# Seven-product blocks in chains of one PSUM bank, and tile 7's second layer in seven products

## Chip, cores and metric

The kernel runs on one core of a Trainium2 chip. The metric is device time in microseconds (us). Of before there are three runs: 278.85, 278.99 and 279.15, median 278.99. A separate profiled execution of it took 279.09 us; its trace spans 277.3 us, counted from the span's start.

## What is computed

Inputs are q, k, v of shape (8, 8, 576, 64) (batch, head, row, depth) and two weight matrices of 512x2048 and 2048x512, all float32.

```python
q_s = softmax(q, axis=-1); k_s = softmax(k, axis=2)
kv  = einsum('bhsd,bhse->bhde', k_s, v)
x   = einsum('bhsd,bhde->bhse', q_s, kv) -> (4608 tokens, 512)
h   = x @ w_in
out = maximum(0.01 * h, h) @ w_out          # (4608, 512)
```

## The kernel before

The 4608 tokens are nine tiles of 512 (TT). xT holds x transposed in bf16, tokens along the free axis. For a tile, layer 1 makes 16 blocks of 128 hidden features: four matmuls (line 562) into a PSUM bank, then `leaky` on ACT (line 571), which writes g in bf16. Layer 2 takes, for each of the tile's four groups of 128 tokens (tsub), 16 matmuls of 512 columns (line 583); ACT copies the bank out and SP issues two stores (`store`, line 575). The attention of the next batches is threaded into tiles 0 to 6 by hooks: `at(t, u, ...)` registers work at step u of tile t, `run(t, u)` emits it. The order on each engine is the order in which the program emits its instructions; engines meet by semaphores alone, and each engine works its queue in order.

The last two tiles, TA = 7 and TB = 8 (counted from 0), are done together after tile 6's layer 1. Seen as two token halves (tile 7, tile 8), two halves of the 512 inputs (CL, CR) and two halves of the 2048 features, layer 1 is a 2x2 by 2x2 block product, and is made with seven products of sums in place of eight (Winograd's form). `token_sums` (line 831) makes s1 to s4 on DVE and a22 on ACT; `in_weight_sums` (line 809) makes t1 to t4 and b22 for each of eight blocks on POOL. All sums and their products are float32r (fp32r in the profile), the plain blocks bf16.

`pair_layer1(i)` (line 978) does block i of eight (NH), features i and 8 + i of both tiles. A product (`product`, line 964) is two matmuls of 512 columns into a PSUM bank of its own. `pair_first` (line 973) makes the first, and ACT copies it out as e1 (line 976). Seven additions on DVE (`add`, line 988) join banks and SBUF partial sums: u2 = p6 + e1, u3 = p7 + u2, e1 + p2, u4 = p5 + u2, c22 = p5 + u3, u3 + p4, u4 + p3. Each of the four results goes through `leaky`. g of tile 7 goes to `g7` (two gj tiles and, from i = 2, places in xT that are no longer needed, `spent`), g of tile 8 to `g8`, also in xT.

Between the products stand `fill` matmuls (`between(n)`, line 1048): 48 matmuls of tile 6's layer 2 and then 16 `pair_step` (line 1023), matmuls of tile 7's layer 2. A block has 14 matmuls of products and 8 fills. After block 7 the other 48 pair steps run (line 1076), while DVE makes the sums r1 to r4 of tile 8's g (lines 1070 to 1074) and ACT copies c22 (line 1069). ACT then copies out and SP stores tile 7. Tile 8's layer 2 is again made in seven products (`product2`, line 1082): 16 matmuls of 256 columns each, the first two bf16, five fp32r with v1 to v4 and o22, sums of w_out made earlier. Its seven additions are at line 1100. Stores (`put`, line 1108) are issued by SP and ACT.

PSUM has eight banks: psB_pool six (tag bank2k), psO_pool two (tag pout).

Of the kernel before, what the change touches and what calls it, by code (L numbers as in the profile page):

```python
# [26 lines left out]
def kernel(  # L27
# [39 lines left out]
    qT_pool = front.enter_context(tc.tile_pool(name="qT", bufs=2))  # L67

# [48 lines left out]
    qe1 = const_pool.tile([P, XE.stop, P], BF16, name="qe1")  # L117
    vb2 = [const_pool.tile([P, R, 2, 2, D + 2], BF16, name=f"vb{i}") for i in range(2)]
# [678 lines left out]
    def out_weight_tiles():  # L797
        for n in ("v1", "v3", "v2", "v4", "o22"):
            late[n] = strip(n).rearrange("p a b -> p (a b)")[:, 0 : NH * H2].rearrange("p (m o) -> p m o", o=H2)
# [9 lines left out]
    def in_weight_sums(i):  # L809
        w = lambda cs, fh: w_in_sb[:, cs, (fh * NH + i) * P : (fh * NH + i + 1) * P]  # L810
        if i == 0:
            late["t"] = strip("t")
# [18 lines left out]
    def token_sums():  # L831
        front.close()
        late["one"] = pool = pairs.enter_context(tc.tile_pool(name="late", bufs=1, reuse_waits="tile"))
# [128 lines left out]
    g8 = spent  # L962

    def product(w, a):
        ps = psB_pool.tile([P, TT], FP32, name="pp", tag=BANK_TAG)
        for c in range(2):
            nc.tensor.matmul(ps, lhsT=w(c), rhs=a(c), start=(c == 0), stop=(c == 1))  # L967
        return ps

    of = lambda n: (lambda c: late[n][:, c])  # L970
    firsts, held_leaky = {}, []

    def pair_first(i):
        firsts[i] = e1 = late["pool"].tile([P, TT], FP32, name="e1")
        ps = product(lambda c: w_in_sb[:, c, i * P : (i + 1) * P], lambda c: xT[:, c, XA])
        nc.scalar.copy(out=e1, in_=ps)

    def pair_layer1(i):
        e1 = firsts[i]
        u2, c22 = (late["one"].tile([P, TT], FP32, name=n) for n in ("u2", "c22"))  # L980
        u3, u4 = (late["pool"].tile([P, TT], FP32, name=n) for n in ("u3", "u4"))
        if i < 2:
            pair = g_pool.tile([P, 2, TT], BF16, name="gj")
            g7[i], g7[NH + i] = pair[:, 0], pair[:, 1]
        else:
            g7[i], g7[NH + i] = (spent(NF + 2 * (i - 2) + n) for n in range(2))

        def add(o, ps, e):
            nc.vector.tensor_tensor(out=o, in0=ps, in1=e, op=ALU.add)  # L989

        p6 = product(of(("t2", i)), of("s2"))
        p7 = product(of(("t3", i)), of("s3"))
        between(2 if i == 0 else 3)
        add(u2, p6, e1)
        for fn in held_leaky:
            fn()
        add(u3, p7, u2)
        p2 = product(lambda c: w_in_sb[:, 2 + c, i * P : (i + 1) * P], lambda c: xT[:, 2 + c, XA])
        add(e1, p2, e1)
        leaky(g7[i], e1)  # L1000
        if i + 1 < NH:
            pair_first(i + 1)
        between(1 if i == 0 else 2)
        p5 = product(of(("t1", i)), of("s1"))
        p4 = product(of(("t4", i)), of("a22"))
        p3 = product(of(("b22", i)), of("s4"))
        between(2 if i == 0 else 3)
        add(u4, p5, u2)
        add(c22, p5, u3)
        if i == 0:  # L1010
            nc.gpsimd.tensor_copy(out=gate, in_=c22[:, 0:1])
        leaky(g8(NH + i), c22)
        add(u3, p4, u3)
        leaky(g8(i), u3)
        add(u4, p3, u4)
        held_leaky[:] = [lambda: leaky(g7[NH + i], u4)]
        if i + 2 < NH:
            in_weight_sums(i + 2)

    pouts, started = {}, [0] * NTS  # L1020
    turn = [j for i in range(NH) for j in (i, NH + i)]

    def pair_step(tsub):
        j = turn[started[tsub]]
        started[tsub] += 1
        if tsub not in pouts:
            pool, tag = (psO_pool, "pout") if tsub < 2 else (psB_pool, BANK_TAG)
            pouts[tsub] = pool.tile([P, O], FP32, name="pout", tag=tag)
        nc.tensor.matmul(  # L1029
            pouts[tsub],  # L1030
            lhsT=g7[j][:, tsub * P : (tsub + 1) * P],
            rhs=w_out_sb[:, j],
            start=(started[tsub] == 1),
            stop=(started[tsub] == NF),
        )
# [17 lines left out]
    between(3)  # L1053
    for i in range(NH):
        pair_layer1(i)
    held_leaky[0]()
    next(fill, None)
    pairs.close()
    pool = ctx.enter_context(tc.tile_pool(name="late3", bufs=1, reuse_waits="tile"))
    quarter = lambda h, b, fh: xT[:, :, (2 * fh + b) * TT + h * M2 : (2 * fh + b) * TT + (h + 1) * M2]  # L1060
    for n in ("r1", "r2", "r3", "r4", "c22"):
        late[n] = pool.tile([P, NH, M2], F32R, name=n)
    for first in (True, False):
        for b in range(2):
            o = lambda n: late[n][:, 4 * b : 4 * b + 4]
            part = lambda n: o(n).bitcast(FP32)
            a11, a12, a21, a22 = (quarter(h, b, fh) for h in range(2) for fh in range(2))
            if first:
                nc.scalar.copy(out=o("c22"), in_=a22)
                nc.vector.tensor_tensor(out=o("r1"), in0=a21, in1=a22, op=ALU.add)  # L1070
                nc.vector.tensor_tensor(out=o("r2"), in0=part("r1"), in1=a11, op=ALU.subtract)
            else:
                nc.vector.tensor_tensor(out=o("r3"), in0=a11, in1=a21, op=ALU.subtract)
                nc.vector.tensor_tensor(out=o("r4"), in0=a12, in1=part("r2"), op=ALU.subtract)

    while started[0] < NF:
        for tsub in range(NTS):
            pair_step(tsub)
    for tsub in range(NTS):
        store(TA * TT + tsub * P, pouts[tsub], nc.scalar.copy)  # L1080

    def product2(a, w, each=False):
        if each:
            ps = [psB_pool.tile([P, H2], FP32, name="pq", tag=BANK_TAG) for _ in range(2)]
        else:
            both = psB_pool.tile([P, 2, H2], FP32, name="pq", tag=BANK_TAG)
            ps = [both[:, 0], both[:, 1]]
        for i in range(2):
            for m in range(NH):
                nc.tensor.matmul(  # L1090
                    ps[i],
                    lhsT=a(m)[:, i * P : (i + 1) * P],
                    rhs=w(m),
                    start=(m == 0 and (each or i == 0)),
                    stop=(m == NH - 1 and (each or i == 1)),
                )
        return ps if each else both

    def add(o, ps, e):
        nc.vector.tensor_tensor(out=o, in0=ps, in1=e, op=ALU.add)  # L1100

    rows = lambda n: (lambda m: late[n][:, m])
    plain_g = lambda fh: (lambda m: g8(fh * NH + m)[:, 0:M2])
    plain_w = lambda fh: (lambda m: w_out_sb[:, fh * NH + m, E1])
    out1, out2 = ([osb_pool.tile([P, O], FP32, name="out_sb") for _ in range(2)] for _ in range(2))
    e1, u2, u3, u4 = (g_pool.tile([P, 2, H2], FP32, name="gu", tag="gj") for _ in range(4))

    def put(o, half, i, cols):
        for n, issue in enumerate((nc.sync, nc.scalar)):
            b, c = divmod(TB * TT + half * M2 + i * P + n * L, S)  # L1110
            issue.dma_start(out=out_r[b, c // L, :, cols], in_=o[n * L : (n + 1) * L, cols])

    nc.scalar.copy(out=e1, in_=product2(plain_g(0), plain_w(0)))
    ps = product2(plain_g(1), plain_w(1))
    for i in range(2):
        add(out1[i][:, E1], ps[:, i], e1[:, i])
        put(out1[i], 0, i, E1)
    add(u2, product2(rows("r2"), rows("v2")), e1)
    add(u3, product2(rows("r3"), rows("v3")), u2)
    ps = product2(rows("r1"), rows("v1"))  # L1120
    for i in range(2):
        add(out2[i][:, E2], ps[:, i], u3[:, i])
    add(u4, ps, u2)
    ps = product2(rows("c22"), rows("v4"), True)
    for i in range(2):
        add(out2[i][:, E1], ps[i], u3[:, i])
        put(out2[i], 1, i, slice(0, O))
    ps = product2(rows("r4"), rows("o22"), True)
    for i in range(2):
        add(out1[i][:, E2], ps[i], u4[:, i])  # L1130
        put(out1[i], 0, i, E2)
# [31 lines left out]
```

## Time and profile before

| what | value |
|---|---|
| median of three runs | 278.99 us |
| profiled execution | 279.09 us, span 277.3 us |
| PE busy | 270.5 us, 98% of the span |
| DVE busy | 221.7 us, 80% |
| ACT busy | 165.4 us, 60% |
| POOL busy | 75.8 us, 27% |
| granted TensorE clock | 1.0 for the whole span |

The time is that of the run; the span is what the trace shows of one execution, some 1.8 us less. PE is TensorE's matmuls, PEld its weight loads, DVE VectorE, ACT ScalarE, POOL GpSimd, SP the engine that issues most DMAs. In a row of the groups, "x32 | 21.4, 688 | 2.9" means 32 instructions, 21.4 us busy together, 688 ns each, 2.9 us idle ahead of them, and then what ended that idle time. A row of the timeline is start, length, engine, line, operation, out<-in, shape and count; "[0.26 <-PE pp L967]" is an idle time ahead of it and what ended it. The length of several pipelined instructions runs from the first's start to the last's end, and so overlaps the next row. The chain that ended last counts from one end to the next, and its pieces don't overlap.

### The profile page before, as it was taken

What the parts mean: (1) busy time and instruction counts of PE and PEld (TensorE: products, weight loads), DVE (VectorE), ACT (ScalarE), POOL (GpSimd) and SP (SyncE); (2) the same over time, 40 slices, a digit from 0 to 9 for tenths busy, and PEclk for the clock granted to TensorE, in tenths of its full rate; (3) what the DMA queues carried; (4) which work ended last, traced back from release to release, by engine and by line L of the source; (5) the groups of instructions that cost most, each with busy time, mean ns of one, the idle gap of its engine ahead of it and who ended that gap; (6) DMA issues with size and microseconds to landing.
All of it is one profiled execution on the core that took longest, in us unless ns stands there. A gap on an engine that the chain in (4) does not pass through costs nothing.

```text
span 277.3 us, 5114 instructions
## 1 busy us (share of the span) xinstructions
PE 270.5 (98%) x1970; PEld 142.6 (51%) x1970; DVE 221.7 (80%) x310; ACT 165.4 (60%) x291; POOL 75.8 (27%) x97
## 2 busy tenths in 40 slices
PE   8799999999999999999999999999999999999994
PEld 3378644444444444445444444454445556564694
DVE  2996995999999949965886498966959998999643
ACT  4976673784489366755486438665673766655300
POOL 2857460259003003100400077003000756600000
PEclk9999999999999999999999999999999999999999
DMA  7999999986995597089408940330601011010253
GB/s 242 334 206 322 244 260 290 392 309 192 272 408 184 66 401 286 2 218 398 136 0 219 406 119 8 85 73 5 162 2 38 0 38 38 9 33 0 57 135 114
DMA packets 40167, 46.46 MB, mean 168 GB/s; under 512 B 18768, under 2 KB 23632, under 8 KB 40144
## 3 DMA queue, kind: packets, MB, share of 16 engines
q1 hardware_dynamic: 36160, 41.43, 47.6%
q0 software_dynamic: 3504, 4.20, 8.8%
q10 hardware_dynamic: 480, 0.52, 0.6%
q8 instruction: 15, 0.25, 0.3%
q14 instruction: 8, 0.07, 0.1%
HBM read 36.70 MB, written 9.44 MB: 166 GB/s over the span
## 4 chain that ended last, share of the span: by engine, by line
PE 91%; DMA 5%; POOL 2%; SPq 0%; DVE 0%; issue 0%
PE pout L583 35%; PE ph L562 33%; PE pp L967 9%; PE pout L1029 5%; PE pq L1090 5%; DMA w_in_sb<-in_moe_w_in_dram 3%; DMA k_raw<-in_k_dram 2%; PE po L478 1%; PE pokv L340 1%; POOL w_in_sb L132 1%; PE pkv L340 1%; POOL vb L217 0%; POOL qe L272 0%; SPq L83 0%; PE pokv L478 0%
## 5 line engine op out<-in xcount | busy, mean ns | idle before, releaser
L583 PE MATMUL pout<-w_out_sb,gj 128*128 128x512 bf16 x448 | 102.6, 380 | 0.0
L562 PE MATMUL ph<-xT,w_in_sb 128*128 128x512 bf16 (+1 forms) x512 | 98.8, 353 | 0.1
L571 ACT ACTIVATE gj<-ph 128x512 bf16<-128x512 f32 x112 | 63.5, 602 | 19.1 <-PE ph L562 18.5
L562 PEld LDWEIGHTS <-w_in_sb 128*128 128x128 bf16 x512 | 49.6, 98 | 47.4 <-DMA w_in_sb<-in_moe_w_in_dram 0.3
L583 PEld LDWEIGHTS <-gj 128*128 128x128 bf16 x448 | 42.1, 98 | 51.5 <-issue 3.5
L217 POOL CAST vb<-v_raw 128x1152 bf16<-128x1152 f32 x13 | 21.1, 1650 | 83.0 <-DMA v_raw<-in_v_dram 83.0
L577 ACT COPY out_sb<-pout 128x512 f32<-128x512 f32 x28 | 16.1, 587 | 41.5 <-PE pout L583 19.2
L320 DVE TENSOR_REDUCE qsum<-qe 128x36 f32<-128x2304 bf16 (+5 forms) x13 | 20.1, 1542 | 6.4 <-ACT qe L311 6.2
L989 DVE TENSOR_TENSOR u<-pp,u 128x512 f32<-128x512 f32 x32 | 21.4, 688 | 2.9 <-PE pp L967 1.3
L205 ACT ACTIVATE ke<-k_raw 128x2304 bf16<-128x2304 f32 (+2 forms) x13 | 18.0, 1383 | 8.2 <-DVE k_raw L197 7.8
L327 DVE TENSOR_TENSOR qe<-qe,qrec 128x2304 bf16<-128x2304 bf16 (+5 forms) x13 | 21.6, 1660 | 0.5
L244 DVE TENSOR_REDUCE qmax<-q_raw 128x36 f32<-128x2304 f32 (+5 forms) x13 | 19.9, 1539 | 0.0
L311 ACT ACTIVATE qe<-q_raw 128x2304 bf16<-128x2304 f32 (+5 forms) x13 | 17.2, 1322 | 3.9 <-POOL q_raw L303 3.0
L197 DVE TENSOR_TENSOR k_raw<-k_raw,kall 128x1152 f32<-128x1152 f32 (+2 forms) x10 | 18.1, 1821 | 0.3
L303 POOL TENSOR_TENSOR q_raw<-q_raw,qmax 128x512 f32<-128x512 f32 (+3 forms) x7 | 11.8, 1680 | 20.5 <-DVE qmax L244 19.3
L967 PE MATMUL pp<-s,t 128*128 128x512 f32 x48 | 16.9, 458 | 0.0
L159 DVE TENSOR_TENSOR t<-t 128x256 f32<-128x256 f32 (+2 forms) x22 | 14.3, 652 | 0.7
L360 DVE RECIPROCAL krec<-pokv 128x2 f32<-128x2 f32 x8 | 1.3, 165 | 16.4 <-PE pokv L478 16.4
L499 ACT CAST xT<-po 128x448 bf16<-128x448 f32 (+3 forms) x31 | 13.3, 515 | 1.3 <-PE po L478 1.3
L789 POOL TENSOR_TENSOR t<-w_in_sb 128x256 fp32r<-128x256 bf16 x16 | 11.4, 715 | 7.6 <-PE pp L967 7.6
L303 DVE TENSOR_TENSOR q_raw<-q_raw,qmax 128x2304 f32<-128x2304 f32 (+1 forms) x6 | 13.2, 2202 | 0.2
L159 DVE TENSOR_TENSOR t<-k_raw 128x512 f32<-128x512 f32 (+1 forms) x11 | 11.2, 1017 | 0.8 <-DMA k_raw<-in_k_dram 0.6
(118 smaller groups left out, 297.4 us busy)
## 6 DMA issues: line engine op xcount, KB each, us to landing
out_dram<-out_sb SPq DMA_DIRECT2D x66, 128.0 KB, 2.8
q_raw<-in_q_dram SPq DMA_DIRECT2D x6, 1152.0 KB, 8.9
v_raw<-in_v_dram SPq DMA_DIRECT2D x6, 1152.0 KB, 11.9
k_raw<-in_k_dram SPq DMA_DIRECT2D x5, 1152.0 KB, 6.7
k_raw<-in_k_dram SPq DMA_DIRECT2D x6, 576.0 KB, 6.0
v_raw<-in_v_dram SPq DMA_DIRECT2D x4, 576.0 KB, 7.6
w_in_sb<-in_moe_w_in_dram POOLq DMA_DIRECT2D x7, 256.0 KB, 7.6
w_out_sb<-in_moe_w_out_dram POOLq DMA_DIRECT2D x6, 256.0 KB, 9.1
```

What stands on the lines that cost most here:

```text
L159: nc.vector.tensor_tensor(out=o, in0=i0, in1=i1, op=ALU.max)
L197: eng.tensor_tensor(out=ks, in0=ks, in1=st[b]["kall"][:, hs].unsqueeze(2).to_broadcast([P, n, R, D]), op=ALU.subtract,)
L217: eng.tensor_copy(out=o, in_=i)
L244: nc.vector.tensor_reduce(out=o, in_=st[b]["q"][:, hs, rs], axis=AX.X, op=ALU.max)
L303: eng.tensor_tensor(out=qs, in0=qs, in1=st[b]["qmax", rs.start, hs.start].unsqueeze(3).to_broadcast([P, m, n, D]), op=ALU.subtract,)
L320: nc.vector.reduce_sum(out=qsum, in_=q_cols(b, rs, hs), axis=AX.X)
L327: nc.vector.tensor_tensor(out=qes if out is None else out, in0=qes, in1=st[b]["qrec", rs.start, hs.start].unsqueeze(3).to_broadcast([P, n, ...
L562: nc.tensor.matmul(ph, lhsT=w_in_sb[:, cb, j * P : (j + 1) * P], rhs=xT[:, cb, c0 : c0 + n], start=(cb == 0 and first), stop=(cb == NB - 1 ...
L571: nc.scalar.activation(out=o, in_=ph, func=AF.Prelu, alpha=LEAKY_SLOPE)
L583: nc.tensor.matmul(pout, lhsT=g_sb[j // 2][:, j % 2, tsub * P : (tsub + 1) * P], rhs=w_out_sb[:, j, os], start=(j == 0), stop=(j == NF - 1),)
L967: nc.tensor.matmul(ps, lhsT=w(c), rhs=a(c), start=(c == 0), stop=(c == 1))
L989: nc.vector.tensor_tensor(out=o, in0=ps, in1=e, op=ALU.add)
```

## The change

Layer 1 of tiles 7 and 8: the products of a block accumulate in PSUM. One bank (px) takes the first, sixth, seventh and fourth product one after another; its partial sums are copied out after the first (e1, ACT), the sixth (u2, DVE) and the seventh (u3, DVE), and the last is read by `leaky` directly. A second bank (py) takes the fifth and the third product. Three additions are left: e1 + pw, u3 + py, u2 + py; the last is held over into the next block. The fills are tile 6's 48 matmuls alone: two ahead, 1 + 2 + 1 in block 0, 2 + 2 + 2 in the others.

Layer 2 of tile 7 has no pair steps any more. It is made in seven products, in turns with those of tile 8, each tile with chains of the same kind: copies by ACT (`snap`), three additions of 256-column halves by DVE. r1 and r3 of tile 7 are summed ahead by POOL (DVE for the last rows), the other row sums by DVE in the end stage, c22 by ACT. The order is written out: first of both tiles, second of both, sixth, fifth, seventh of tile 7, sixth of tile 8, fourth, third of tile 7, seventh, fifth, fourth, third of tile 8.

For room in SBUF qe1 and vb move to a pool that ends with the attention, a pool "late0" for r3 and r1 is opened ahead of the others, and t takes the first strip of the raw pool.

```diff
-    qe1 = const_pool.tile([P, XE.stop, P], BF16, name="qe1")
+    qe1 = fix_pool.tile([P, XE.stop, P], BF16, name="qe1")
...
+    def sums_ahead(n):
...
+        (ms, h0), (_, h1) = g7_blocks(0)[n], g7_blocks(1)[n]
+        for name, x, y, op in (("r1", h1(0), h1(1), ALU.add), ("r3", h0(0), h1(0), ALU.subtract)):
+            eng = nc.vector if n == 3 else nc.gpsimd
+            eng.tensor_tensor(out=late[name][:, ms], in0=x, in1=y, op=op)
...
+    def product(ps, w, a, first=True):
         for c in range(2):
-            nc.tensor.matmul(ps, lhsT=w(c), rhs=a(c), start=(c == 0), stop=(c == 1))
+            nc.tensor.matmul(ps, lhsT=w(c), rhs=a(c), start=(first and c == 0), stop=(c == 1), skip_group_check=True)
...
+    def pair_layer1(i, fills):
+        px, e1 = firsts[i]
...
+        product(px, of(("t2", i)), of("s2"), False)
+        for fn in held:
+            fn()
+        nc.vector.tensor_copy(out=u2, in_=px)
+        pw = bank()
+        product(pw, lambda c: w_in_sb[:, 2 + c, i * P : (i + 1) * P], lambda c: xT[:, 2 + c, XA])
+        if i + 1 < NH:
+            pair_first(i + 1)
+        add(e1, pw, e1)
+        leaky(g7[i], e1)
+        between(fills[0])
+        product(px, of(("t3", i)), of("s3"), False)
+        nc.vector.tensor_copy(out=u3, in_=px)
+        py = bank()
+        product(py, of(("t1", i)), of("s1"))
+        between(fills[1])
+        add(u3, py, u3)
+        leaky(g8(NH + i), u3)
...
+        product(px, of(("t4", i)), of("a22"), False)
+        leaky(g8(i), px)
+        between(fills[2])
+        product(py, of(("b22", i)), of("s4"), False)
+        held[:] = [lambda: add(u2, py, u2), lambda: leaky(g7[NH + i], u2)]
         if i + 2 < NH:
             in_weight_sums(i + 2)
+        if i in (2, 4, 6):
+            sums_ahead(i // 2 - 1)
...
-        for tsubs in ((2, 3), (0, 1)):
-            for _ in range(4):
-                for tsub in tsubs:
-                    pair_step(tsub)
-                    yield
...
+    def snap(z, n):
+        z[n] = gu()
+        if z["each"]:
+            for i in range(2):
+                nc.scalar.copy(out=z[n][:, i], in_=z["x"][i])
+        else:
+            nc.scalar.copy(out=z[n], in_=z["xx"])
...
+    def sixth(z):
+        product2(z["x"], rows("r2"), rows("v2"), z["each"], first=False)
+        snap(z, "u2")
...
+    first(A)
+    sums(A, "r2")
+    first(B8)
+    sums(A, "r4")
+    sums(A, "c22")
+    second(A)
+    c11(A)
+    second(B8)
+    sixth(A)
+    fifth(A)
+    late["r1"] = strip("r1").rearrange("p a b -> p (a b)")[:, 0 : NH * M2].rearrange("p (m t) -> p m t", t=M2)
+    for (ms, _), (_, h1) in zip(g8_wide(0), g8_wide(1)):
+        nc.vector.tensor_tensor(out=late["r1"][:, ms], in0=h1(0), in1=h1(1), op=ALU.add)
+    c11(B8)
+    sums(B8, "r2")
+    seventh(A)
+    A["o2"], B8["o2"] = out_pairs(), last_pairs("o2")
+    sixth(B8)
+    c22(A)
+    fourth(A)
+    sums(B8, "c22")
+    third(A)
+    sums(B8, "r3")
+    seventh(B8)
+    fifth(B8)
+    c12(A)
+    sums(B8, "r4")
+    c22(B8)
+    fourth(B8)
+    third(B8)
+    c12(B8)
```

In the new code A is tile 7 and B8 tile 8.

More of the change, by code (lines that the diff above doesn't have):

```diff
@@ L973, in pair_first @@
+    firsts, held = {}, []
     def pair_first(i):
-        firsts[i] = e1 = late["pool"].tile([P, TT], FP32, name="e1")
-        ps = product(lambda c: w_in_sb[:, c, i * P : (i + 1) * P], lambda c: xT[:, c, XA])
+        ps, e1 = bank(), keep("e1")
+        product(ps, lambda c: w_in_sb[:, c, i * P : (i + 1) * P], lambda c: xT[:, c, XA])
         nc.scalar.copy(out=e1, in_=ps)
[L978 to L995, printed above, removed]
-            fn()
[L997 to L1000, printed above, removed]
@@ L1052 @@
     pair_first(0)
-    between(3)
+    between(2)
     for i in range(NH):
-        pair_layer1(i)
-    held_leaky[0]()
+        pair_layer1(i, (2, 2, 2) if i else (1, 2, 1))
+    for fn in held:
+        fn()
     next(fill, None)
+    sums_ahead(3)
     pairs.close()
[L1059 to L1062, printed above, removed]
@@ L1099, in add @@
[L1099 to L1111, printed above, removed]
@@ L1113 @@
[L1113 to L1131, printed above, removed]
+    last_pool = ctx.enter_context(tc.tile_pool(name="late3", bufs=1, reuse_waits="tile"))
+    def banks2(each=False, pool=psB_pool, tag=BANK_TAG):
+        if each:
+            return [pool.tile([P, H2], FP32, name="pq", tag=tag) for _ in range(2)]
+        both = pool.tile([P, 2, H2], FP32, name="pq", tag=tag)
+        return [both[:, i] for i in range(2)]
@@ new lines, in product2 @@
+    def product2(ps, a, w, each=False, turns=False, first=True):
+        order = [(i, m) for i in range(2) for m in range(NH)]
+        if turns:
+            order = [(i, m) for m in range(NH) for i in range(2)]
+        for i, m in order:
+            nc.tensor.matmul(
+                ps[i],
+                lhsT=a(m)[:, i * P : (i + 1) * P],
+                rhs=w(m),
+                start=(first and m == 0 and (each or i == 0)),
+                stop=(m == NH - 1 and (each or i == 1)),
+                skip_group_check=True,
+            )
@@ new lines, in second, with fifth, seventh, fourth @@
+    def second(z):
+        z["w"] = banks2(False, psO_pool, "pout")
+        product2(z["w"], plain_g(z["g"], 1), plain_w(1), turns=True)
+    def sixth(z):
+        product2(z["x"], rows("r2"), rows("v2"), z["each"], first=False)
+        snap(z, "u2")
+    def fifth(z):
+        z["y"] = banks2(z["each"])
+        product2(z["y"], rows("r1"), rows("v1"), z["each"])
+    def seventh(z):
+        product2(z["x"], rows("r3"), rows("v3"), z["each"], first=False)
+        snap(z, "u3")
+    def fourth(z):
+        product2(z["x"], rows("c22"), rows("v4"), z["each"], first=False)
+        for i in range(2):
+            nc.scalar.copy(out=z["o2"][i][:, E1], in_=z["x"][i])
+            put(z, z["o2"][i], 1, i, slice(0, O))
@@ new lines, in third, with c11, c22, c12 @@
+    def third(z):
+        product2(z["y"], rows("r4"), rows("o22"), z["each"], first=False)
+    def c11(z):
+        for i in range(2):
+            add(z["o1"][i][:, E1], z["w"][i], z["e1"][:, i])
+            put(z, z["o1"][i], 0, i, E1)
+    def c22(z):
+        for i in range(2):
+            add(z["o2"][i][:, E2], z["y"][i], z["u3"][:, i])
+    def c12(z):
+        for i in range(2):
+            add(z["o1"][i][:, E2], z["y"][i], z["u2"][:, i])
+            put(z, z["o1"][i], 0, i, E2)
+    def sums(z, n):
+        pool = late["ahead"] if n == "r3" else last_pool
+        row_sums(z["wide"], n, n, pool, *dict(
+            r2=(ALU.subtract, "r1", (0, 0)),
+            r3=(ALU.subtract, (0, 0), (1, 0)),
+            r4=(ALU.subtract, (0, 1), "r2"),
+            c22=(None, (1, 1), None),
+        )[n])
```

137 lines of the change are left out of this document (72 added, 65 removed).

## The prediction

> **What bounds the kernel now.** I read the chain that ended last first, then the windows of the end, then the rows of single engines. The chain is nearly all PE:
>
> ```profile
> PE 91%; DMA 5%; POOL 2%; SPq 0%; DVE 0%; issue 0%
> ```
>
> Windows for the four stretches the change touches: block 0 of tile 8's layer 1, blocks 1 to 7, the rest of tile 7's layer 2, the seven products of tile 8's layer 2. Columns: stretch, its length, busy time and count of PE, PEld, DVE, ACT, POOL, then granted clock, DMA share, GB/s.
>
> ```profile
> 210.84:215.59 4.75, 4.72 (x22) 2.63 (x20) 4.64 (x7) 1.26 (x4) 0.00 (x0) 1.00 0.24 55
> 215.59:249.49 33.90, 33.90 (x153) 20.00 (x151) 31.17 (x50) 21.68 (x39) 17.92 (x31) 1.00 0.10 24
> 249.49:260.51 11.02, 11.02 (x53) 5.04 (x52) 10.85 (x11) 4.46 (x7) 0.00 (x0) 1.00 0.01 1
> 260.51:277.30 16.79, 13.08 (x113) 12.54 (x110) 5.38 (x12) 2.03 (x4) 0.00 (x0) 1.00 0.47 125
> ```
>
> PE is busy 33.90 of 33.90 us in blocks 1 to 7 and DVE 31.17: DVE is near full, but PE never waits for it. So DVE work that goes frees nothing by itself. What can shorten the end is less PE work; what can lengthen it is a PE instruction that has to wait. One block and the end in the chain (start, length, engine, tile, line, matmuls):
>
> ```profile
> 238.66 1.40 PE pp L967 x6
> 240.05 0.66 PE pout L583 x3
> 240.72 0.93 PE pp L967 x4
> 241.65 0.66 PE pout L1029 x3
> 242.31 0.86 PE pp L967 x4
> 243.18 0.43 PE pout L1029 x2
> 243.61 1.38 PE pp L967 x6
> 249.49 11.02 PE pout L1029 x51
> 260.51 13.10 PE pq L1090 x112
> ```
>
> A bf16 matmul of 512 columns takes 0.86/4 = 0.216 us of the stream (0.218 in the fills, 0.66/3), an fp32r one 0.93/4 = 0.2323. The 112 of 256 columns divide by their starts:
>
> ```profile
> 260.35 3.66 PE L1090 MATMUL pq<-w_out_sb,xT 128*128 128x256 bf16 x32
> 263.76 6.00 PE L1090 MATMUL pq<-v,r 128*128 128x256 f32 x48
> 269.60 2.08 PE L1090 MATMUL pq<-v,c 128*128 128x256 f32 x16
> ```
>
> (269.60 - 263.76)/48 = 0.121 each in fp32r, 0.108 in bf16. Seven products are therefore 32 x 0.108 + 80 x 0.1206 = 13.1 us, against 64 x 0.216 = 13.8 us for a plain layer 2.
>
> **Part 1: the PE work.** Out go 64 plain matmuls of tile 7's layer 2, 16 in the fills and 48 after them: 16 x 0.218 + 48 x 0.216 = 13.86 us. In come seven products: 13.10 us. Layer 1 keeps its 14 matmuls a block. Gain **0.76 us**, the largest that the change can bring. The fills fall from eight to six a block; a block without waits is 4 x 0.216 + 10 x 0.2323 + 6 x 0.218 = 4.50 us.
>
> **Part 2: what a wait of an fp32r matmul costs.** The chains in one bank bring waits that before did not have: a product may add to the bank only when the copy of what is there has been read. Before has one stop of this kind, at block 0, where the seventh product waited for s3 (DVE, line 789):
>
> ```profile
> 210.62 1.22 DVE L789 TENSOR_TENSOR s<-xT 128x1024 fp32r<-128x1024 bf16 x1
> 211.96 0.30 PEld L967 LDWEIGHTS pp<-s,t 128*128 128x128 f32 x2 [0.44 <-issue]
> 211.99 0.47 PE L967 MATMUL pp<-s,t 128*128 128x512 f32 x1
> ```
>
> s3 ends at 211.84; the weights, which had long been there, load only at 211.96; the matmul ends at 212.46. So the stop holds the weight load too: release 0.12 us, then 0.50 us to the end of the first matmul. Another release:
>
> ```profile
> 10.59 0.28 DVE L393 TENSOR_REDUCE kr<-kT 128x2 f32<-128x128 f32 x1
> 10.93 0.44 PE L398 MATMUL kallp<-identf,kr 128*64 128x128 f32 x4 [0.31 <-DVE kr L393]
> ```
>
> 10.93 - 10.87 = 0.06. I take 0.08, between 0.06 and 0.12: a matmul that waits ends 0.58 us after what it waits for. For 256 columns:
>
> ```profile
> 263.73 0.19 PEld L1090 LDWEIGHTS pq<-v,r 128*128 128x128 f32 x1
> 263.76 0.36 PE L1090 MATMUL pq<-v,r 128*128 128x256 f32 x1
> ```
>
> From the load's start to the matmul's end 0.39, so 0.08 + 0.39 = 0.47.
>
> **Part 3: the copies.** The trace has the same copy, PSUM to SBUF on DVE, at another line, and the add it replaces:
>
> ```profile
> L577 DVE COPY out_sb<-pout 128x512 f32<-128x512 f32 x4 | 2.5, 682 | 0.0
> L989 DVE TENSOR_TENSOR u<-pp,u 128x512 f32<-128x512 f32 x32 | 21.4, 688 | 2.9 <-PE pp L967 1.3
> ```
>
> A copy costs what an add does. DVE falls from seven such operations a block to five, which pays nothing, but two of the five now stand between two products. How soon DVE starts, and how close two follow each other:
>
> ```profile
> 243.16 0.68 DVE L989 TENSOR_TENSOR e<-pp,e 128x512 f32<-128x512 f32 x1
> 244.10 0.69 DVE L989 TENSOR_TENSOR u<-pp,u 128x512 f32<-128x512 f32 x1 [0.26 <-PE pp L967]
> 244.71 0.68 DVE L989 TENSOR_TENSOR c<-pp,u 128x512 f32<-128x512 f32 x1
> ```
>
> The fifth product is the first two of the six matmuls at 243.61 and ends at 244.07: DVE starts 0.03 later, and the next operation follows after 0.61.
>
> *u3, then the fourth product.* From the end of the seventh product: DVE starts at 0.04, ends at 0.73, the first matmul of the fourth ends at 0.73 + 0.58 = 1.31. PE's work between is the fifth product and two fills; unstopped, that matmul would end at 0.465 + 0.436 + 0.232 = 1.13. **Stop 0.18 us, eight times: 1.44.** Behind it stand the rest of the PE queue and all that comes later.
>
> *u2, then the seventh.* From the end of the block before: the held add starts at 0.04, the copy at 0.65, ends at 1.34, plus 0.58 = 1.92. Unstopped: sixth 0.465, second and next first 0.864, two fills 0.436, 0.232 = 2.00. No stop in blocks 1 to 6, by 0.08. In block 7 there is no next first (0.432): **0.35**.
>
> *u3's add, then the third.* The add ends 0.73 later than the copy, at 1.46, plus 0.58 = 2.04; the third's first matmul stands, after the stop, at 1.31 + 0.232 + 0.436 + 0.232 = 2.21. Nothing.
>
> **Block 0.** Three operations that were not in PE's way before now are:
>
> ```profile
> 210.41 0.43 PE pp L967 x2
> 210.93 0.59 ACT L976 COPY e<-pp 128x512 f32<-128x512 f32 x1
> 212.89 0.69 DVE L989 TENSOR_TENSOR u<-pp,e 128x512 f32<-128x512 f32 x1
> ```
>
> The sixth product now waits for ACT's copy e1 (to 211.52): first matmul at 212.10 where 210.84 + 0.436 + 0.232 = 211.51 was possible, **0.59**. The copy u2 stands on DVE behind s1 to s4, so where the add stood, 212.89 to 213.58: the seventh's first matmul at 214.16 against 212.33 + 0.864 + 0.218 + 0.232 = 213.64, **0.52**. The third's wait for u3's add costs **0.05**. The old wait for s3 goes: 212.46 against 211.96 + 0.232, **-0.27**.
>
> **Part 4: the end.** Tile 7 and 8 in turns are 64 bf16 and 160 fp32r matmuls. DVE has to make r2, r4 of tile 7 and r1, r2 of tile 8 before the sixth product of tile 8, at these prices:
>
> ```profile
> 252.53 1.23 DVE L1071 TENSOR_TENSOR r<-r,xT 128x1024 fp32r<-128x1024 f32 x1
> 253.67 1.22 DVE L1070 TENSOR_TENSOR r<-xT 128x1024 fp32r<-128x1024 bf16 x1
> 269.80 0.76 DVE L1100 TENSOR_TENSOR out_sb<-pq,gu 128x256 f32<-128x256 f32 x2 [1.23 <-PE pq L1090]
> ```
>
> ```profile
> L571 ACT ACTIVATE xT<-u 128x512 bf16<-128x512 f32 x14 | 8.4, 627 | 0.8 <-DVE u L989 0.8
> ```
>
> One after another they take 1.14 for 1024 elements (253.67 - 252.53), 0.61 for 512 as above, and 0.34 for 256 (0.76 for two against 0.42 for the single one at this line). From the end of layer 1: held add and leaky (0.63) to 1.43; the last r1, r3 1.21; r2 and r4 of tile 7 in pieces of 512, 1024, 512, 2.35 each; c11 0.68; r1 2.28; c11 0.68; r2 of tile 8 2.36: **13.34**. PE has done four bf16 products (6.91), three fp32r (5.79) and four matmuls (0.48) by 13.18, and the fifth would end at 13.30; it ends at 13.34 + 0.47 = 13.81: **0.51**. After that DVE stays ahead: tile 8's r3 follows 3.1 us later (13.34 + 0.68 + 2.36 = 16.4), and the product that reads it starts at about 19.0; r4 is done 2.7 us before the last product. ACT's snapshots (0.59, as for e1) have a whole product (1.93) to hide behind. POOL's six new sums are bounded by
>
> ```profile
> L272 POOL TENSOR_TENSOR qe<-qe,qrec 128x512 bf16<-128x512 bf16 x1 | 1.0, 1041 | 0.0
> 239.21 0.68 POOL L789 TENSOR_TENSOR t<-w_in_sb 128x256 fp32r<-128x256 bf16 x1 [1.91 <-PE pp L967]
> ```
>
> that is 2.1 us more in three blocks, against 1.9 us that POOL waits in each and a block of lead; without that cover block 5 or 7 would pay the difference, 0.2 us. The stores of tile 7 move into the products; what follows the last matmul (add of 256 columns, two stores a half) is the same as before. Moving qe1, vb2 and t changes only which finished tiles the late ones lie on; all readers of those come before s1 on their engines, so nothing is priced.
>
> **Sum.** -0.76 - 0.27 + 0.59 + 0.52 + 1.44 + 0.05 + 0.35 + 0.51 = **+2.4 us**. The profiled execution took 279.09 us with a span of 277.3; the median shown is 278.99, 0.1 below, and I put the sum on it: **281.4 us**. Every 0.01 us of release counts eleven times: releases of 0.03 and 0.12 give +1.9 and +2.9, 280.9 to 281.9.
>
> **Rivals.** *A, the weight load goes ahead of the wait.* Then a stopped matmul ends 0.40 (its own length) and not 0.50 after the release; the stops fall, in the order of the sum and with a release of 0.05, to 0.46 + 0.52 + 0.40 + 0.05 + 0.22 + 0.38, with none to 0.41 + 0.52 + 0 + 0.04 + 0.17 + 0.35. Less 1.03 that is +1.0 and +0.5: 279.5 to 280.0. For it: unstopped loads do run beside the matmul before. Against it: the load at 211.96. The Trainium skill, in TensorE: Matmul & The Clock Gate, section Step-by-step: what each phase is for, says that PE's queue pulls weight loads ahead of matmuls in flight when they go to the background buffer. By that rule it would be A; the one row here that shows a wait disagrees.
>
> *B, faster.* The change pays if no product finds its copy unfinished: the stop of 0.18 lies only that far over the edge, and one fill more between (0.218) would close it. Then the PE bill alone counts, and block 0 must lose its two stops as well: 278.99 - 0.76 = 278.2. It decides at a copy of 0.50 us; the row has 0.682. Against it also: block 0's 1.1 us hang on DVE's queue, not on this edge.
>
> *C, DVE's run at the end is longer.* From layer 1's end DVE works 11.9 us with no gap, and all that it loses there delays tile 8's sixth product one for one. The trace has SBUF operations of one shape at two prices:
>
> ```profile
> L159 DVE TENSOR_TENSOR t<-t 128x256 f32<-128x256 f32 x11 | 6.7, 606 | 0.3
> L303 DVE TENSOR_TENSOR q_raw<-q_raw,qmax 128x256 f32<-128x256 f32 x1 | 0.4, 425 | 0.0
> ```
>
> A tenth on 11.9 us is 1.2 us: 282.6. Against it: POOL has nothing to do then, and the r rows of before ran at one price.
>
> *D, the change doesn't do what it says:* excluded for the operations, since the built kernel has two copies and three adds a block on DVE; open only for time, which is B.
>
> **How the numbers follow.** Forecast 0.60, A 0.17, C 0.12, B 0.06, 0.05 for what I have not seen. The range takes in A and C and leaves out B: 279.5 to 282.8. About 0.2% (0.56 us) is what a measurement of this kernel tells from no change, so same is 278.43 to 279.55: the low end of A and a share of the unseen, 0.08; faster 0.07 (B and a little unseen); slower 0.85.
>
> **What would show it.** Right: blocks 4.65 to 4.7 us apart; PEld idle with "issue" before the weights of the fourth product in each block; block 0's last product near 216.6 and layer 1's near 249.3; sixth product of tile 8 waiting about half a us for DVE; span about 279.7. Wrong: blocks 4.5 apart with no idle before the fourth product (A or B); DVE copies clearly under 0.6; gaps on PE in the end other than that one; POOL's weight sums late before a sixth product.

## The result and the profile after

| | before | after |
|---|---|---|
| median | 279.02 us (278.85 to 279.15, 4 runs) | 282.59 us (281.84 to 282.73, 4 runs) |
| profiled execution, span | 279.09, 277.3 | 282.73, 280.9 |
| first matmul of the pair stage starts | 210.25 | 210.76 |
| last matmul ends | 273.61 | 276.90 |
| between the two | 63.36 | 66.14 |
| last matmul to the span's end | 3.69 | 4.00 |

After is slower by the ratio 1.0123, interval [1.0104, 1.0142]. The forecast was 281.4. The profiled execution is 3.6 us longer: **2.78** in the stretch that the change rewrites (forecast +2.4), 0.3 behind the last matmul, and 0.5 by a later start of that stretch. The last two were in no term of the sum. Spans are known to 0.1 us, so what is given behind the last matmul holds to 0.05.

The windows of after, cut at the ends of the first product, of block 0, of layer 1 and of the last matmul; the columns are those of the windows of before.

```profile
211.35:217.29 5.94, 5.30 (x22) 2.53 (x20) 4.70 (x6) 2.71 (x6) 0.78 (x2) 1.00 0.21 47
217.29:250.35 33.06, 32.91 (x141) 17.26 (x140) 22.91 (x35) 20.96 (x37) 23.73 (x36) 1.00 0.08 17
250.35:276.90 26.55, 26.45 (x224) 25.34 (x222) 19.78 (x28) 10.46 (x21) 0.00 (x0) 1.00 0.31 72
276.90:280.90 4.00, 0.00 (x0) 0.00 (x0) 0.42 (x1) 0.00 (x0) 0.00 (x0) 0.82 0.44 121
```

Blocks 1 to 7 have 12 matmuls fewer than before, in the count that the trace shows (141 against 153), and last 33.06 us against 33.90: 0.84 less, where 14 fills at 0.218 (two in each of seven blocks) would be 3.05 less. PE looks busy in 32.91 of the 33.06, for the record of a matmul that waits for its weights gets longer and counts as busy: those of the fourth product take up to 0.499 us in after, at most 0.398 in before. DVE fell from 31.17 to 22.91. Busy time does not show this loss; the places of the instructions do. One block of after in the chain that ended last:

```profile
226.29 1.81 PE pp L1012 x8
228.10 0.43 PE pout L584 x2
228.53 0.94 PE pp L1012 x4
229.46 0.45 PE pout L584 x2
229.91 0.66 PE pp L1012 x2
230.57 0.45 PE pout L584 x2
231.02 1.81 PE pp L1012 x8
```

From 226.29 to 231.02 it is 4.73 us. The four matmuls of the seventh and fifth product take 0.94, 0.235 each; the two of the fourth product take 0.66 where two take 0.465. That is the stop, **0.20** a block. Its cause stands in the timelines of DVE, PEld and PE, block 1 of after:

```profile
219.57 0.69 DVE L1043 COPY u<-pp 128x512 f32<-128x512 f32 x1 [0.35 <-PE pp L1012]
220.37 0.69 DVE L1015 TENSOR_TENSOR u<-pp,u 128x512 f32<-128x512 f32 x1
```

```profile
220.32 0.30 PEld L1012 LDWEIGHTS pp<-a,t 128*128 128x128 f32 x2 [0.37 <-DVE u L1043]
```

```profile
220.32 0.73 PE L1012 MATMUL pp<-a,t 128*128 128x512 f32 x2
```

The copy u3 ends at 220.26. The weights of the fourth product, on SBUF since long before, load 0.06 later. They do not load at the start of the two fills, at 219.84, though PEld has nothing to do for 0.37 us. The weight load waits with its matmul, so the stop holds both.

The late start comes in this execution from far ahead, from tile 0. Row of the costliest groups, after:

```profile
L563 PE MATMUL ph<-xT,w_in_sb 128*128 128x512 bf16 (+1 forms) x512 | 98.8, 352 | 0.3 <-DMA w_in_sb<-in_moe_w_in_dram 0.3
```

PE waited there for a piece of w_in. In the timelines about 31 us the second layer of tile 0 starts 0.53 later than in before (31.61 against 31.08), and all that follows keeps this:

```profile
31.08 2.11 PE L583 MATMUL pout<-w_out_sb,gj 128*128 128x512 bf16 x9
```

```profile
31.61 1.67 PE L584 MATMUL pout<-w_out_sb,gj 128*128 128x512 bf16 x7
```

It differs from execution to execution: ten other kernels of this study have the same code up to the pair stage, and their starts lie between 210.06 and 210.94. Where the profiled start was 210.76 to 210.94, that run was 0.7 to 0.9 us above the lowest of the same kernel (282.73 with 281.84 beside it; 282.75 with 282.09 to 282.15; 281.17 with 280.44 to 280.70). The piece of w_in is not the only source. After again (start 210.87) and three mends (210.94), both below, begin the second layer of tile 0 at 31.19 and 31.07, much as before does; from the start of tile 1's second layer to the first matmul of tile 2 they then take 15.66 and 15.99 where before takes 15.32, and in three mends PE waits 0.22 there for POOL (vb, line 218). What makes some executions late in tile 1, and whether the moved places have a part in it, no run here settles. What is compared below is therefore, beside the times, the stretch from the pair stage's first matmul to the last matmul, which does not depend on it.

### The profile page after: what moved, and what is told of

It is laid out like the page before. It is cut to its first block, busy times and chain, and to the rows that moved or that the text cites. A ratio compares the mean times of both kernels' runs of the same rounds, so it can differ in the third digit from the quotient of the medians.

```text
span 280.9 us, 5223 instructions
## 1 busy us (share of the span) xinstructions
PE 273.1 (97%) x2018; PEld 147.7 (53%) x2018; DVE 216.8 (77%) x303; ACT 170.2 (61%) x302; POOL 81.2 (29%) x103
## 5 line engine op out<-in xcount | busy, mean ns | idle before, releaser
L584 PE MATMUL pout<-w_out_sb,gj 128*128 128x512 bf16 x448 | 103.7, 380 | 0.0
L218 POOL CAST vb<-v_raw 128x1152 bf16<-128x1152 f32 x13 | 19.8, 1551 | 83.7 <-DMA v_raw<-in_v_dram 66.4
L578 ACT COPY out_sb<-pout 128x512 f32<-128x512 f32 x24 | 14.0, 584 | 34.8 <-PE pout L584 18.0
L1015 DVE TENSOR_TENSOR u<-pp,u 128x512 f32<-128x512 f32 x16 | 11.1, 692 | 8.6 <-PE pp L1012 7.8
L1012 PE MATMUL pp<-s,t 128*128 128x512 f32 x48 | 14.9, 419 | 0.8 <-issue 0.3
L572 ACT ACTIVATE xT<-u 128x512 bf16<-128x512 f32 x14 | 8.8, 630 | 10.9 <-DVE u L1015 10.8
```

What stands on the lines that cost most here:

```text
L218: eng.tensor_copy(out=o, in_=i)
L572: nc.scalar.activation(out=o, in_=ph, func=AF.Prelu, alpha=LEAKY_SLOPE)
L584: nc.tensor.matmul(pout, lhsT=g_sb[j // 2][:, j % 2, tsub * P : (tsub + 1) * P], rhs=w_out_sb[:, j, os], start=(j == 0), stop=(j == NF - 1),)
L1012: nc.tensor.matmul(ps, lhsT=w(c), rhs=a(c), start=(first and c == 0), stop=(c == 1), skip_group_check=True)
```

## The experiments

| kernel | median, us | ratio to before, interval | pair stage's first matmul to the last one | last matmul to span's end |
|---|---|---|---|---|
| before | 279.02 | 1 | 63.36 | 3.69 |
| after | 282.59 | 1.0123 [1.0104, 1.0142] | 66.14 | 4.00 |
| after again | 282.13 | 1.0121 [1.0106, 1.0136] | 66.13 | 4.00 |
| places only | 279.20 | 1.0010 [1.0001, 1.0019] | 63.38 | 3.74 |
| chains in layer 1 only | 280.91 | 1.0076 [1.0062, 1.0090] | 65.10 | 3.74 |
| seven products only | 281.85 | 1.0106 [1.0092, 1.0119] | 65.51 | 3.99 |
| fills 2, 3, 1 | 281.56 | 1.0095 [1.0082, 1.0109] | 65.33 | 3.99 |
| fills 2, 1, 3 | 283.74 | 1.0174 [1.0159, 1.0189] | 67.63 | 3.93 |
| s4 on POOL | 281.65 | 1.0101 [1.0084, 1.0117] | 65.58 | 4.02 |
| r4 late | 281.94 | 1.0112 [1.0097, 1.0127] | 65.79 | 3.98 |
| three mends | 280.52 | 1.0050 [1.0038, 1.0062] | 64.48 | 3.98 |
| one chain a block | 279.92 | 1.0038 [1.0023, 1.0052] | 63.60 | 3.99 |
| copy first | 278.91 | 0.9994 [0.9980, 1.0008] | 62.78 | 3.94 |

The before that runs beside each lay at 278.88 to 279.02. The theory: each stop of PE is paid by itself, since PE is the one chain, and the stops at copies cost more than the saved fills. Its rivals: the moved places, the end stage, or a weight load that does go ahead (A).

**Places only.** Before, with the three moved places alone (t's in out_weight_tiles).

```diff
-    qe1 = const_pool.tile(...)
-    vb2 = [const_pool.tile(...) for i in range(2)]
+    qe1 = fix_pool.tile(...)
+    vb2 = [fix_pool.tile(...) for i in range(2)]
...
+        late["t"] = strip("t")
```

> Before with the moved places alone: qe1 and vb in the pool that ends with the attention, t in the first strip; every product as before. In the profile of after, layer 1 of the last two tiles starts 0.51 us later than in before (first product ends at 211.35, not 210.84). Theory (the waits for copies are the cost, the late start is chance): no change, within 0.3 us of before, start near 210.8. Rival (the places delay the front part): +0.5 us, start near 211.35.

The stretch is 63.38 against 63.36; the time is 0.2 above, at the edge of what can be told. The places are not the cause of what the stretch loses.

**Chains in layer 1 only.** Before with the moved places and the new product chains in layer 1; the second layer of tile 7 stays plain, so there are eight fills a block.

```diff
...
-        pair_layer1(i)
+        pair_layer1(i, (2, 3, 3) if i else (1, 2, 2))
```

> Chains in one bank in layer 1 alone; tile 7's layer 2 stays plain, so each block has eight fills, 2 + 3 + 3. Theory: the third fill (0.22) covers the stop of 0.18 to 0.20 ahead of the fourth product, so blocks 1 to 6 run at 4.93 us as before; left are the stops of block 0 (0.37 + 0.52 + 0.18 + 0.05 - 0.27 = 0.85) and of block 7 (0.35): +1.2 us. Rival (chains cost by themselves, in matmuls that add to a bank or in releases that fills don't cover): 4.93 + 0.2 us a block, +2.5 us or more.

The stretch grows by 1.74, more than the 1.2 expected and less than the 2.5 of the rival. One of blocks 1 to 6, in the chain that ended last:

```profile
226.22 1.80 PE pp L981 x8
228.02 0.43 PE pout L584 x2
228.45 0.93 PE pp L981 x4
229.38 0.66 PE pout L584 x3
230.05 0.47 PE pp L981 x2
230.52 0.67 PE pout L584 x3
231.19 1.81 PE pp L981 x8
```

With three fills ahead of it the fourth product takes 0.47: no stop. The blocks are 4.97 apart, 4.95 in before (238.66 to 243.61). So a third fill covers the copy, and what is left of the cost lies in block 0 (about 1.0, expected 0.85) and in block 7, where the seventh product waits 0.6 us for the copy u2 (expected 0.35). That copy starts at 247.44, when the second product ends, and not 0.61 after the held addition (246.57), as it does in after (245.72 and 246.33); why, no run shows. The chains alone cost 1.9 us of time and bring nothing to PE.

**Seven products only.** Layer 1 as in before, seven banks and seven additions, but with six fills; the new end.

```diff
-        between(2 if i == 0 else 3)
+        between(1 if i == 0 else 2)
...
+        if i in (2, 4, 6):
+            sums_ahead(i // 2 - 1)
```

> Tile 7's layer 2 in seven products as in after, but layer 1 with a bank for each product and seven additions as in before, six fills a block. Theory: no product waits for a copy, so layer 1 runs at 4.50 to 4.55 us a block with DVE at 4.3 of it; PE work -0.76; at the end DVE has two more additions to do before its row sums, so the sixth product of tile 8 waits about 1.4 us: +0.6 us in all. Rival (DVE is the bound once fills go): blocks of 4.65 us or more, +1.5 us or more.

My expectation of +0.6 fell: 2.8 us slower, nearly as much as the whole change. PE runs layer 1 without a stop, blocks 4.51 apart. The bill comes at its end, in the chain:

```profile
246.82 0.45 PE pout L584 x2
247.27 1.76 PE pq L1092 x16
249.03 0.68 DVE u L1022
...
262.88 13.23 PE pq L1092 x108
```

PE ends layer 1 at 247.27 and then has to wait for DVE. The timeline of DVE, block 0's first addition, block 7's first two and its last:

```profile
213.23 0.68 DVE L1022 TENSOR_TENSOR u<-pp,e 128x512 f32<-128x512 f32 x1
...
241.06 0.68 DVE L1022 TENSOR_TENSOR u<-pp,e 128x512 f32<-128x512 f32 x1
...
245.63 0.68 DVE L1022 TENSOR_TENSOR u<-pp,e 128x512 f32<-128x512 f32 x1
...
249.01 1.29 DVE L1022 TENSOR_TENSOR u<-pp,u 128x512 f32<-128x512 f32 x2
```

Block 0's additions start only when s4 is made, at 213.23, and seven additions take 4.57 a block (241.06 to 245.63) where PE now goes 4.51: DVE never makes up its late start. In before, with blocks of 4.95, it had 0.38 a block to do so. Its last additions end at 250.30, 3.0 after PE's layer 1; in after the last one ends 0.7 after it. By these 2.3 us the row sums r2 and r4 are later, and the end takes 28.84 us where it takes 26.55 in after. So the fills of before were DVE's cover too, and with seven additions a block in this order the saved PE work is lost again. "DVE work that goes frees nothing by itself" held for before only.

**Fills 2, 3, 1 and 2, 1, 3.** After, with one fill moved to ahead of the fourth product, and one moved away from it.

```diff
-        pair_layer1(i, (2, 2, 2) if i else (1, 2, 1))
+        pair_layer1(i, (2, 3, 1) if i else (1, 2, 1))
```

> After with the six fills of blocks 1 to 7 placed 2 + 3 + 1 and not 2 + 2 + 2; nothing else. Theory: one fill more between the seventh and the fourth product closes that stop (0.20 measured), and the third product still finds its addition done (by 0.01): blocks of 4.53 in place of 4.73 us, 1.3 to 1.4 us faster than after, about +2.2 us on before. Rival (the stop only moves to the third product): no gain over after, +3.5 us on before.

> After with the six fills of blocks 1 to 7 placed 2 + 1 + 3: one fill less between the seventh and the fourth product. Theory (the fourth product waits for the copy u3, whatever PE does meanwhile): the stop grows by the fill's 0.22, blocks of 4.95 us in place of 4.73, +1.5 us on after, about +5.0 us on before. Rival (what costs is the chain in one bank, not the time for the copy): no difference from after.

With one more fill the stretch falls by 0.81, with one less it grows by 1.49, which is 0.21 a block, the length of a fill. Cost and cover move together, as a stop on one chain should. But the gain is only some half of the stops in the seven blocks that were edited, 7 x 0.20 = 1.4; 1.3 to 1.4 was expected. A block of fills 2, 3, 1 in the chain:

```profile
229.47 0.47 PE pp L1012 x2
229.94 0.23 PE pout L584
230.16 1.89 PE pp L1012 x8
```

The fourth takes 0.47, it doesn't stop any more; but the eight matmuls that start with the third product take 1.89, in after 1.81. With a fill less ahead of it, the third product now waits for u3's add: 0.08 in each of seven blocks, 0.6 in all, is what is missing. The forecast let that add end 0.73 after the copy; by the DVE rows of after (219.57 and 220.37) it starts 0.80 after the copy's start and ends 0.80 after its end. An addition that reads what the operation ahead of it writes starts 0.11 us after its end; one that doesn't starts 0.08 *before* it (0.61 apart at a length of 0.69).

**After again.** The same kernel with no edit.

> After unchanged, with a second profile. Theory (the late start of 0.51 us in the first profile is the time at which w_in arrived in that execution): start of the pair stage between 210.8 and 211.4, its time about +3.3 us on before. Rival (it belongs to the kernel): start at 211.35 again, +3.6 us.

282.13, with the profiled run at 282.75 and a start at 210.87: the stretch is 66.13, as in the first. The start is late again, but in the three runs that were not profiled the time is 0.6 lower, and the lateness is not that of w_in (above).

**s4 on POOL.** After, block 0's last sum of tokens moved off the queue in which the copy u2 stands.

```diff
-        subtract(nc.vector, "s4", xT[:, CR, XA], plain("s2"))
+        subtract(nc.gpsimd, "s4", xT[:, CR, XA], plain("s2"))
```

> After with s4 made by POOL, which waits for block 0 then, and not by DVE ahead of the copy u2. Theory (in block 0 the seventh product waits for the copy, and the copy for DVE's queue of sums): the copy starts at the end of the sixth product, 0.5 us sooner, and so the rest: 0.5 us faster than after. Rival (POOL and DVE slow each other's sums, or s4 now comes too late for the third product): no gain, or a loss of up to 0.7.

Down by 0.56. Timelines, of DVE in after, then of POOL and of DVE in this kernel:

```profile
212.25 1.22 DVE L790 TENSOR_TENSOR s<-xT,s 128x1024 fp32r<-128x1024 bf16 x1
213.39 0.68 DVE L1034 COPY u<-pp 128x512 f32<-128x512 f32 x1
```

```profile
210.77 3.01 POOL L790 TENSOR_TENSOR s<-xT,s 128x1024 fp32r<-128x1024 bf16 x1 [19.67 <-issue]
```

```profile
212.31 0.69 DVE L1034 COPY u<-pp 128x512 f32<-128x512 f32 x1 [0.54 <-PE pp L1012]
```

The copy starts at 212.31 and now waits for PE, not for DVE's queue. Counted from the first matmul of the pair stage it starts at 2.11 (212.31 - 210.20) where it was 2.63 (213.39 - 210.76), 0.52 sooner; 0.52 was the forecast's term for "the copy u2 stands on DVE behind s1 to s4".

**r4 late.** After, tile 7's r4 made behind tile 8's r2, which lies in a place of its own.

```diff
-    sums(A, "r4")
...
...
-    sums(B8, "r2")
...
+    row_sums(g8_wide, "r2", "r2b", last_pool, ALU.subtract, "r1", (0, 0))
...
+    sums(A, "r4")
...
```

> After with DVE making r4 of tile 7 behind r2 of tile 8 (in a place of its own) and not ahead of it; tile 8's first output halves lie in free gj places for room. Theory (the sixth product of tile 8 waits for DVE's run of sums): that gap, 0.3 us of idle weight loads in after, closes: 0.3 us faster than after. Rival (the end is bound by PE alone): no difference.

Down by 0.35. The wait stands in the timeline of PEld in after; it isn't there in this kernel, whose 224 matmuls of the end take 26.21 us. That is 64 x 0.108 + 160 x 0.1206, so no stop is left in the end.

```profile
257.08 6.30 PEld L1093 LDWEIGHTS pq<-v,r 128*128 128x128 f32 x52
263.67 0.41 PEld L1093 LDWEIGHTS pq<-v,r 128*128 128x128 f32 x3 [0.29 <-DVE r L1110]
```

**Three mends.** Fills 2, 3, 1, s4 on POOL and r4 late (its diff above) together.

```diff
-        subtract(nc.vector, "s4", ...)
+        subtract(nc.gpsimd, "s4", ...)
...
-        pair_layer1(i, (2, 2, 2) if i else (1, 2, 1))
+        pair_layer1(i, (2, 3, 1) if i else (1, 2, 1))
```

> The changed kernel with three of its stops taken away together: fills 2, 3, 1 in blocks 1 to 7, s4 of block 0 made by POOL, and tile 7's r4 made behind tile 8's r2. Theory (each stop of PE is paid by itself, one after the other on one chain): the three single runs shortened pair stage and end by 0.81, 0.53 and 0.34 us in their traces, so together 1.7 us off the changed kernel: about 280.4, which is still 1.4 above the kernel before. Of those 1.4 the rest of the stops (third product 0.10 a block, block 0, block 7's seventh) makes about 1.9, the 0.3 behind the last matmul comes on top, and the saved PE work takes 0.76 off. Rival (the stops share a cover, so that taking one away brings out the next): POOL's or DVE's work becomes late elsewhere and the sum is clearly less than the three gains, 281.2 or more. The time tells them apart at about 280.8; in the trace, layer 1's end at 248.5 and a tail of 26.2.

The stretch falls by 1.66; the three alone made 0.81 + 0.56 + 0.35 = 1.72. The stops add up: they are paid one by one. The time is 280.52, 1.6 above the before beside it (278.95).

**One chain a block.** If stops at copies are the loss and seven additions the other wall, a form between them should pay: only the first and the sixth product share a bank, ACT copies u2, DVE does six additions and no copy, and two of block 0's fills go ahead of it. The end is that of "r4 late".

```diff
+        product(px, of(("t2", i)), of("s2"), False)
+        p7 = bank()
+        product(p7, of(("t3", i)), of("s3"))
         between(fills[0])
+        nc.scalar.copy(out=u2, in_=px)
+        for fn in held:
+            fn()
+        add(u3, p7, u2)
+        p2 = bank()
...
+        p5, p4, p3 = bank(), bank(), bank()
+        product(p5, of(("t1", i)), of("s1"))
+        product(p4, of(("t4", i)), of("a22"))
+        product(p3, of(("b22", i)), of("s4"))
```

> Another way to make tile 7's seven products: of a block's products only the first and the sixth share a PSUM bank, the copy of it (u2) is made by ACT, the other five products have banks of their own with six additions on DVE in all, four fills a block and the rest ahead of block 0; the end is that of the run with r4 late. Theory (the loss of the changed kernel is its stops of PE at copies, and DVE's count of operations a block sets whether layer 1 keeps up): without a stop on the fourth, third and seventh product the blocks go 4.50 apart, the fills saved are worth 0.76, block 0 keeps about 0.2 for the sixth product's wait, the end keeps the 0.3 behind the last matmul and up to 0.3 for DVE's lag: 278.5 to 279.5, even with the kernel before. Rival 1 (six additions make DVE's period longer than PE's, as seven additions did): DVE falls behind in layer 1 and PE waits 1 us or more in the end: 280 to 281. Rival 2 (ACT's copy is late, so u3's add and what follows is late): PE stops for a bank in layer 1, blocks above 4.6, 280 or more.

279.92 misses the expectation by 0.4. All blocks but one go 4.51 apart; once the chain leaves PE:

```profile
235.21 0.02 issue
235.23 0.58 ACT out_sb L578
235.81 0.50 ACT u L1036
236.31 0.02 issue
236.34 0.69 DVE u L1015
237.03 0.61 DVE e L1015
237.64 0.02 issue
237.66 0.02 ACT xT L572
237.68 0.51 issue
238.19 0.58 ACT e L1024
238.77 0.14 issue
238.91 1.17 PE pp L1012 x4
```

A finished output tile is copied out by ACT just there, ahead of u2's copy, and the lateness goes through five operations to the sixth product of the next block. That is rival 2, in one block of eight.

**Copy first.** The same with u2's copy ahead of the two fills in the program's order.

```diff
-        between(fills[0])
         nc.scalar.copy(out=u2, in_=px)
+        between(fills[0])
```

> The run with one chain a block once more, with the copy u2 on ACT set ahead of the two fills and not behind them. In the trace of that run PE stopped once, for about 0.8 us, in block 6: ACT had the copy of a finished output tile of tile 7 (0.58 us, waiting for the second fill) in its queue ahead of u2's copy, and u2's add, u1's add, the leaky and the next copy e1 came late one after the other, up to the sixth product that waits for e1. Theory: with u2's copy first that chain starts at the end of the sixth product and the stop goes: 0.8 less, 279.1, the same as the kernel before within 0.3; blocks 4.51 apart throughout and layer 1's end at about 246.9 where 247.7 was. Rival (the copy of the output tile is itself what is late, and holds up the leaky of that block in the same way): the stop stays above 0.4 us, 279.5 or more.

278.91, ratio 0.9994 [0.9980, 1.0008]; the stop is gone (62.78 against 63.60). The same place on ACT:

```profile
234.34 0.59 ACT L1035 COPY u<-pp 128x512 f32<-128x512 f32 x1
235.20 0.59 ACT L578 COPY out_sb<-pout 128x512 f32<-128x512 f32 x1 [0.28 <-PE pout L584]
```

The stretch is 0.58 shorter than before's, 0.18 short of the forecast's gain of 0.76 on PE. The sixth product waits for the copy e1 in two blocks, 0.18 in block 0 and 0.23 in block 1, while the old wait of 0.27 for s3 is gone; 0.76 - 0.18 - 0.23 + 0.27 is 0.62. So that gain is real. The 0.2 to 0.3 us behind the last matmul (3.94 against 3.69) eats nearly half of it, the moved places perhaps 0.2, and in the time nothing that can be told from before is left. No kernel here beats before.

## Why the prediction was right, and where its sizes were off

The direction, the mechanism and its places were right; the forecast was 1.2 us short of 282.6, and 0.7 short of the 282.13 of after again. That the time lies inside the range is partly luck: the spread that the forecast gave for its own mechanism, 280.9 to 281.9, holds neither time, and the range reaches up to 282.8 only for rival C, which did not come about. By the steps:

- **"Gain 0.76 us" of PE work:** right. With most stops removed the stretch is 0.58 shorter than before's (copy first).
- **"Stop 0.18 us, eight times":** 0.20. With it, the fills behind an fp32r product take 0.45 for two and not 0.436, and the blocks are 4.73 apart, not "4.65 to 4.7". Blocks 1 to 7 take 33.06 us; from the forecast's 216.6 to 249.3 it was 32.7. **+0.36**, the largest mis-sized term.
- **Block 0:** the sixth product's first matmul ends at 212.60, 1.25 after the first product (forecast 212.10 - 210.84 = 1.26); the seventh's at 214.69, 3.34 after it (forecast 3.32). Both terms, 0.59 and 0.52, hold. The block's last product ends 5.94 after the first product, not 5.76: **+0.18**. Half of it is the rounding of "near 216.6", for the terms by themselves give 216.7; the rest is the fourth's and the third's stop.
- **"u3's add, then the third ... Nothing":** right in after, by a margin thinner than 2.21 against 2.04, since the add starts 0.11 after the copy's end and not 0.08 before it. It shows when the stop ahead of it goes (fills 2, 3, 1), and so **rival B's** "one fill more between would close it" was wrong too: it closes that stop and opens half of another.
- **Block 7's 0.35:** right (0.13 and 1.16 for four matmuls that take 0.93, in the chain of after: 0.36).
- **The end, 0.51:** 0.34, **-0.17**. The end takes 26.55, and 26.21 without a stop. Rival C, a longer DVE run, is out: the run took 13.26 us (250.35 to 263.61) where 13.34 was summed.
- **Rival A** is out: the load at 220.32 follows the copy's end at 220.26. The Trainium skill's rule, in TensorE: Matmul & The Clock Gate, section Step-by-step: what each phase is for, is that weight loads are pulled ahead of matmuls in flight. The trace agrees only from the release on: the load at 220.32 starts before the second fill ends (220.44), but not before the copy has ended, so for an fp32r matmul that waits the rule does not give what rival A took from it. The prediction's row against A, the load at 211.96, could not show this by itself, since the product ahead ended at 211.96 too (211.49 and 0.47 in before's chain).

These three differences, +0.36 + 0.18 - 0.17, make 0.37, and 2.43 + 0.37 = 2.80 against 2.78 measured. What the sum did not have is 0.3 behind the last matmul, some 0.2 that the moved places may cost (priced at nothing; in the time of places only, not in its stretch), and the late start, which the profiles of after, after again and three mends show.

The **0.3 behind the last matmul** stays unexplained. The last packets are stored equally late after it; the busy shares of the DMA engines, before in 40 slices of 0.0575 us from 275.0, after in slices of 0.0725 from 278.0:

```profile
DMA  4123288589996720000000000000000000000000
```

```profile
DMA  7862423489979972000000000000000000000000
```

Before has its last packets by slice 16, 275.92, 2.31 after the last matmul, and 1.4 to the end; after has them by about slice 17, 279.2, 2.3 after, and 1.7 to the end. The extra lies behind the last store. The table has it in every kernel with the new end (3.93 to 4.02) and in no other (3.69 to 3.74). No run here tells what it is.

## What to carry to other kernels

A chain of products in one accumulator saves additions, not waits: each copy between two products puts copy, release, weight load and matmul one after another on TensorE's own chain, and only work between them that does not wait for the copy covers that. Count that cover product by product, with the dependent start of the second operation, before the additions saved are counted. When work is taken from the bounding engine, work out the period of the next one in the same stretch: here fills that looked like plain work were the cover of VectorE's seven additions, and the bill came 15 us later.

## What the runs showed of the hardware that was not expected

- An fp32r matmul that waits holds its weight load too: the load starts 0.06 us (220.26 to 220.32) to 0.12 us (214.07 to 214.19) after the release, and a matmul of 512 columns ends 0.50 after the load's start.
- VectorE starts an operation of 512 elements 0.61 us after the one ahead where it does not read that one's result, and 0.80 after it where it does (both 0.69 long).
- GpSimd took 3.01 us for a sum of 1024 elements for which VectorE takes 1.22.
- The start of the last stage can shift by 0.5 to 0.7 us from one execution to another, in after with the arrival of one weight piece, and the shift stays to the end: TensorE, 97% busy, has no slack in which to lose it.
